# Buffers of the first expert's rows and of the side splits, and the engines that evacuate the output, in an attention and MoE kernel

## The chip, the cores and the metric

The kernel runs on one core of a Trainium2 chip, as one launch. The metric is the time of one execution on the device in microseconds; here it is given as the median of several runs. The engines that matter: TensorE (PE) multiplies into PSUM; ScalarE (ACT), VectorE (DVE) and GpSimd (POOL) copy, add and round; SyncE (SP) issues every DMA of this stage, in one queue and in program order. Each engine works through its own instructions in order, and waits on semaphores where an operand is not there or a buffer is not free.

## The reference

```python
def reference(**kwargs):
    attn_out = _attn_ref(**attn_kwargs)      # 4 x 8 x 576 x 64, window of 64
    x = ascontiguousarray(attn_out.transpose(0, 2, 1, 3)).reshape(2304, 512)
    return _moe_ref(x=x, **moe_kwargs)

def _moe_ref(x, w_gate, w1, w2):
    P = exp(x @ w_gate - max)                # 2304 x 8
    for _ in range(8):                       # Sinkhorn: rows, columns
        P /= P.sum(1, keepdims=True) + 1e-09
        P /= P.sum(0, keepdims=True) + 1e-09
        P *= N / E
    out = zeros((N, D))
    for e in range(8):                       # dense: all rows, all experts
        h = maximum(x @ w1[e], 0.0)          # 512 -> 1024
        out += P[:, e:e + 1] * (h @ w2[e])   # 1024 -> 512
    return out
```

## The kernel before

**Arithmetic.** Every product of 32-bit numbers is made of three products of rounded high and low parts; a "split" of a tile is a cast of its high part (ScalarE) and a subtraction for its low part (POOL). The two products of each expert are made by the seven-product scheme of Strassen and Winograd; the steps of a block are numbered 1 to 7 after the products and run in the order 1, 5, 6, 2, 7, 3, 4.

**Passes.** The 2304 rows are 18 tiles of 128, and three passes take six tiles each. Pass 0 splits the weights as it needs them and stores the splits of w1 in DRAM (w1d), and half of the combinations of w2 (w2d). Half of the first expert is computed in the attention phase already; its rows (yd, 128 x 512 a tile) are scaled by the gate and added when the outputs of a pass are finished. Only the passes 1 and 2 and the two places where a pass meets the next concern us.

**The flow of a pass.** First blocks F[0] to F[29] (L217: x times w1, TensorE; then scaling, rounding to a buffer G, three of them) and Second blocks S[u][0], S[u][1] for fifteen units u (L1148: G times w2 into the accumulator acc). The flow is F0; F1, F2, S0; F3, F4, S1; ...; F29, S14, and the last steps of a block are interlaced with the first of the next. In First.step, a product is copied from PSUM by ScalarE: qb (L1048) after product 1, p (L1053) after 5, u (L1060) after 6, r (L1070) after 2. A bank is written again three or four products later, so a late copy stops TensorE.

**Weights of S.** A unit needs seven parts of w2, each 128 x 512. load_w2 loads a raw part on SP into the ring wr (four buffers, L978); split_w2 casts it (L741, ScalarE) and subtracts it (L742, POOL) into one of eight split buffers (wp, w2c); the next split that comes up in the program issues the load owed for a buffer that has come free. w1's splits of F[i+2] are loaded by five DMAs after step 4 of F[i] (L754), and a change of expert brings two more (pb, the gate's row, L722).

**Side splits.** Pass 2's unit 0 takes its seven w2 parts already split, from w2keep in DRAM. Pass 1 makes them, one in each of the units 2 to 8: keep_split takes a raw part (a wr buffer) and a second wr buffer for its high half, casts (L998), subtracts (L999), and stores both (L1001), and the two buffers are loaded again once the stores have landed.

**Meetings.** Where one pass ends and the next begins, TensorE transposes each of six output tiles (turn, L1224) into a PSUM bank, and finish (L1233, VectorE) makes one operation of scaling the tile's first-expert row and adding the bank to it; flush stores it. At the second meeting (pass 1 to 2) rows 0 to 3 are loaded into the G buffer in which the next x stood (new_x, load_x, high L1250, low L1253), rows 4 and 5 into the two ys buffers. At the first meeting there is no first-expert row to add, and acc is stored as it stands (out_rows, L1209). At the end of pass 2 the last tiles are finished in pieces (even_tiles, after_last).

**Order.** It is written out by hand: hook(block, step) hangs a call behind a step of a block, prior does so for the next pass, and bulk and urgent are queues from which a step takes one or all.

Of the kernel before, what the change touches and what calls it, by code (L numbers as in the profile page):

```python
# [8 lines left out]
F32 = mybir.dt.float32  # L9
# [12 lines left out]
def window_attention_sinkhorn_moe(ctx: ExitStack, tc: tile.TileContext, q, k, v, w_gate, w1, w2, out):  # L22
# [300 lines left out]
    with tc.manual_schedule():  # L323
# [617 lines left out]
        with ExitStack() as p3:  # L941
# [19 lines left out]
            KEEP = {u: k for u, k in zip(range(2, 9), ORDER)}  # L961
            seq = []
            for p in range(1, NPASS):
                for u in range(n_units):
                    if p == 1 or u:
                        seq += [(p, u, k) for k in ORDER]
                    if p == 1 and u in KEEP:
                        seq += [("raw", 0, KEEP[u]), ("high", 0, KEEP[u])]
# [3 lines left out]
            def load_w2():  # L972
# [3 lines left out]
                t = new("wr", [P, 2, HD], F32R, 4)  # L976
                if p != "high":
                    nc.sync.dma_start(out=f32(t), in_=w2_block(u, part) if part < 3 else w2d[u][:, part - 3])  # L978
                R[p, u, part] = t

# [7 lines left out]
            def split_w2(p, u, part):  # L988
                while owed:
                    owed.pop(0)()  # L990
                W[p, u, part] = split_into(new_wp(), f32(R.pop((p, u, part))))
                owed.append(load_w2)

            def keep_split(part):
                while owed:
                    owed.pop(0)()
                r, h = R.pop(("raw", 0, part)), R.pop(("high", 0, part))
                nc.scalar.copy(out=h, in_=f32(r))  # L998
                nc.gpsimd.tensor_tensor(out=r, in0=f32(r), in1=f32(h), op=ALU.subtract)  # L999
                for x, t in enumerate((h, r)):  # L1000
                    nc.sync.dma_start(out=w2keep[part][:, :, x, :], in_=f32(t))  # L1001
                owed.extend([load_w2, load_w2])
# [208 lines left out]
            def load_y(p, ts, own=False):  # L1211
                for t in ts:
                    ys[t] = new("ys", [P, DM], F32, 2) if own else side["x"][:, ORDER[t]].rearrange("p k c -> p (k c)")[:, 0:DM]
                    nc.sync.dma_start(out=ys[t], in_=yd[FIRST[p] + t])

            ys, yps = {}, {}
# [15 lines left out]
            def finish(p, t, cols):  # L1232
                nc.vector.scalar_tensor_tensor(  # L1233
                    out=ys[t][:, cols], in0=ys[t][:, cols], scalar=prob[:, FIRST[p] + t, 0:1], in1=yps[t][:, cols], op0=ALU.mult, op1=ALU.add)
# [22 lines left out]
            next_pb(1, 1)  # L1257
            first = plans[0][1][0]
# [4 lines left out]
            for p, F, S, flow in plans:  # L1263
# [146 lines left out]
```

## Time and profile before

| | us |
|---|---|
| median of three runs | 1571.19 |
| fastest, slowest | 1570.77, 1574.69 |
| the profiled execution, its own time | 1571.05 |
| its span | 1569.3 |
| TensorE busy | 1549.7 (99%) |
| VectorE, POOL busy | 966.6 (62%), 985.3 (63%) |
| ScalarE busy | 759.3 (48%) |

The span is what the profiler recorded between the first and the last instruction; 1.75 us of the execution's own time lie around it. A busy TensorE is counted by its records, whose ends are modelled, so a group can seem to overlap with the next; the time of a product is better read from start to start. Pass 1 runs from about 668 us, the first meeting lies there, the second meeting is at about 1096 to 1160 us, and the last product ends at 1565.

### The profile page before, as it was taken

To read this page: it belongs to the slowest core of one execution; us is meant where nothing else is said; L and a number is where in the kernel's file an instruction comes from. 1 tells how busy PE (TensorE), PEld (TensorE's weight loads), DVE (VectorE), ACT (ScalarE), POOL (GpSimd) and SP (SyncE) were. 2 spreads that over 40 slices of the span, in tenths; PEclk is the share of its full clock that TensorE was granted. 3 is DMA by queue.
4 is the path that set the end of the run, shared out by engine and by line. 5 is a ranking of instruction groups with operands and counts; after the bars stand their busy time and mean duration, and the time that the engine had idled before them with its cause. 6 is when DMAs were issued, how large, how long until landed. Compare 5 with 4: busy or idle time off the path is not lost.

```text
span 1569.3 us, 26783 instructions
## 1 busy us (share of the span) xinstructions
PE 1549.7 (99%) x9665; PEld 1475.7 (94%) x9665; DVE 966.6 (62%) x1799; ACT 759.3 (48%) x1667; POOL 985.3 (63%) x920
## 2 busy tenths in 40 slices
PE   8999999999999999999999999999999999999998
PEld 7888889988998998899999999999999999999998
DVE  6666566575455455655665665665746566566666
ACT  6666535443443344355545545444454454454452
POOL 6244467677767677356676676566557666667564
PEclk9999999999999999999999999999999999999999
DMA  9876467567756765895666666665966566566562
GB/s 222 197 172 150 137 227 285 207 221 264 266 208 242 261 220 200 293 318 167 226 231 202 223 228 202 198 208 184 337 210 211 174 202 212 171 208 209 168 195 101
DMA packets 231233, 335.67 MB, mean 214 GB/s; under 512 B 70162, under 2 KB 153214, under 8 KB 227134
## 3 DMA queue, kind: packets, MB, share of 16 engines
q1 hardware_dynamic: 231102, 333.97, 65.7%
q8 instruction: 76, 1.25, 0.3%
q14 instruction: 55, 0.45, 0.1%
HBM read 236.34 MB, written 90.63 MB: 208 GB/s over the span
## 4 chain that ended last, share of the span: by engine, by line
PE 90%; DMA 4%; DVE 3%; ACT 2%; issue 1%; POOL 1%; SPq 0%; DVEq 0%; ACTq 0%
PE qb L217 17%; PE y L276 15%; PE qc L217 11%; PE qa L217 11%; PE qb L1148 10%; PE qa L1148 7%; PE qc L1148 7%; PE hp L562 3%; PE yp L576 3%; PE vp L479 1%; DMA w1c<-w1d 1%; PE sp L410 1%; PE tp L390 1%; PE tp L464 1%; DMA w2keep<-wr 1%
## 5 line engine op out<-in xcount | busy, mean ns | idle before, releaser
L217 PE MATMUL qb<-xc,w1c 128*128 128x384 f32 x1620 | 321.9, 336 | 4.1 <-ACT u L1060 3.5
L1034 POOL TENSOR_TENSOR G<-sm,G 128x384 fp32r<-128x384 f32 x176 | 179.2, 1018 | 186.3 <-ACT G L1030 186.3
L217 PEld LDWEIGHTS qb<-xc,w1c 128*128 128x128 f32 x1620 | 284.6, 188 | 6.3 <-ACT u L1060 5.1
L276 PE MATMUL y<-w2c,g 128*128 128x512 f32 x1080 | 251.2, 391 | 0.5 <-DVE acc L295 0.5
L276 PEld LDWEIGHTS y<-w2c,g 128*128 128x128 f32 x1080 | 201.8, 188 | 42.6 <-DVE acc L295 0.9
L217 PE MATMUL qa<-xc,w1c 128*128 128x384 f32 x1080 | 213.3, 337 | 0.2 <-DMA w1c<-w1d 0.2
L217 PE MATMUL qc<-xc,w1c 128*128 128x384 f32 x1080 | 213.0, 336 | 0.0
L217 PEld LDWEIGHTS qa<-xc,w1c 128*128 128x128 f32 x1080 | 190.4, 188 | 1.7 <-DMA w1c<-w1d 0.5
L217 PEld LDWEIGHTS qc<-xc,w1c 128*128 128x128 f32 x1080 | 190.1, 188 | 0.0
L1156 DVE TENSOR_TENSOR acc<-qb,acc 128x384 f32<-128x384 f32 x171 | 95.1, 556 | 123.8 <-PE qb L1148 116.8
L742 POOL TENSOR_TENSOR w2c<-wr,w2c 128x512 fp32r<-128x512 f32 x99 | 126.7, 1296 | 48.0 <-ACT w2c L741 38.0
L178 POOL TENSOR_TENSOR w2c<-stg,w2c 128x512 fp32r<-128x512 f32 x60 | 84.6, 1431 | 108.4 <-PE qb L217 95.8
L742 POOL TENSOR_TENSOR wp<-wr,wp 128x512 fp32r<-128x512 f32 x100 | 127.9, 1298 | 39.2 <-ACT wp L741 31.2
L1030 ACT CAST G<-sm 128x384 fp32r<-128x384 f32 x180 | 92.2, 513 | 65.7 <-DVE sm L1041 65.7
L1148 PE MATMUL qb<-G,w2c 128*128 128x384 f32 x552 | 111.4, 336 | 2.6 <-ACT qb L1162 2.6
L1148 PE MATMUL qb<-G,wp 128*128 128x384 f32 x528 | 106.5, 336 | 0.1
L1148 PEld LDWEIGHTS qb<-G,w2c 128*128 128x128 f32 x552 | 97.7, 188 | 2.9 <-ACT qb L1162 2.9
L295 DVE SCALAR_TENSOR_TENSOR acc<-y,prob,acc 128x512 f32<-128x512 f32 x72 | 54.0, 749 | 69.2 <-PE y L276 68.5
L1148 PEld LDWEIGHTS qb<-G,wp 128*128 128x128 f32 x528 | 93.5, 188 | 0.4 <-DVE G L1034 0.4
L1156 DVE TENSOR_TENSOR acc<-qc,acc 128x384 f32<-128x384 f32 x116 | 64.4, 555 | 41.3 <-PE qc L1148 40.7
L458 POOL TENSOR_TENSOR s<-s,rr 128x512 f32<-128x512 f32 x36 | 37.5, 1041 | 79.8 <-DVE rr L457 71.1
L1041 POOL TENSOR_TENSOR r<-sm,r 128x384 f32<-128x384 f32 x60 | 61.1, 1019 | 30.8 <-ACT u L1060 23.2
(205 smaller groups left out, 2918.0 us busy)
## 6 DMA issues: line engine op xcount, KB each, us to landing
w1c<-w1d SPq DMA_DIRECT2D x120, 512.0 KB, 6.4
w1d<-w1c SPq DMA_DIRECT2D x30, 1792.0 KB, 7.7
w1c<-w1d SPq DMA_DIRECT2D x180, 256.0 KB, 3.4
stg<-in_moe_w_dram SPq DMA_DIRECT2D x66, 512.0 KB, 4.2
wr<-w2d SPq DMA_DIRECT2D x118, 256.0 KB, 3.2
wr<-in_moe_w_dram SPq DMA_DIRECT2D x88, 256.0 KB, 3.2
w2d<-tf SPq DMA_DIRECT2D x30, 512.0 KB, 4.8
vs<-v SPq DMA_DIRECT2D x35, 128.0 KB, 4.2
```

The source lines that it names most:

```text
L178: nc.gpsimd.tensor_tensor(out=w[:, 1], in0=src[:, j], in1=f32(w[:, 0]), op=ALU.subtract)
L217: nc.tensor.matmul(bank, lhsT=w[:, ws, a, kk, :], rhs=xc[xs][:, b, kk, :], start=(first and j == 0), stop=(j == 5), skip_group_check=not f ...
L276: nc.tensor.matmul(yp, lhsT=g[:, a, o:o + P], rhs=w[:, x, :], start=(i == 0), stop=(i == 11))
L295: nc.vector.scalar_tensor_tensor(out=at, in0=yp, scalar=pr, in1=at, op0=ALU.mult, op1=ALU.add)
L562: nc.tensor.matmul(hp, lhsT=w1s[c][:, a, kk, :], rhs=xs[j][:, b, kk, :], start=(i == 0), stop=(i == 3 * KD - 1))
L576: nc.tensor.matmul(yp, lhsT=g[:, a, o * P:(o + 1) * P], rhs=w[:, x, :], start=(i == 0), stop=(i == 11))
L742: nc.gpsimd.tensor_tensor(out=t[:, :, 1, :], in0=r, in1=f32(t[:, :, 0, :]), op=ALU.subtract)
L1030: nc.scalar.copy(out=self.g[:, k, 0, :], in_=src)
L1034: eng.tensor_tensor(out=self.g[:, k, 1, :], in0=src, in1=f32(self.g[:, k, 0, :]), op=ALU.subtract)
L1041: eng.tensor_tensor(out=dst, in0=x, in1=y, op=op)
L1148: nc.tensor.matmul(bank, lhsT=W[p, u, wp][:, g, y, cols], rhs=G7[p, 2 * u + g][:, gp, x, :], start=(start and j == 0), stop=(j == 5), skip ...
L1156: nc.vector.tensor_tensor(out=at, in0=src, in1=at, op=ALU.add)
```

## The change

It alters five places.

1. The side splits take the two ys buffers in place of two wr buffers, and are three calls: the load behind step 4 of F[2u+2], the cast and the subtraction behind step 7 of S[u][0] (in before, taken from the queue bulk), the stores behind step 2 of S[u][1].
2. At the second meeting rows 2 to 5 lie in the wr ring, which then holds nothing else (the loads for pass 2's unit 1 are taken out and come back behind steps of F2), rows 0 and 1 in ys. The tiles turn in the order 2, 3, 4, 5, 0, 1, one step or more apart from before. Tiles 5 and 1 ("a") are copied by ScalarE from PSUM into the place of acc that they came from, their rows are scaled by POOL (scale_row) and added by POOL.
3. Of the next x, part 0 is rounded behind S[14][0].1 in place of S[14][1].1.
4. At the first meeting three of the six stores of acc are issued before the first block, and the split of w2 part 5 goes from F1.3 to F2.5.
5. At the end of the program tile 0's last three quarters are copied by ScalarE and added by POOL ("p"), in place of VectorE's one operation, and the whole row of that tile is scaled by POOL beforehand.

```diff
             KEEP = {u: k for u, k in zip(range(2, 9), ORDER)}
+            WR_ROWS = (2, 3, 4, 5)
             seq = []
             for p in range(1, NPASS):
                 for u in range(n_units):
                     if p == 1 or u:
                         seq += [(p, u, k) for k in ORDER]
-                    if p == 1 and u in KEEP:
-                        seq += [("raw", 0, KEEP[u]), ("high", 0, KEEP[u])]
+                if p + 1 < NPASS:
+                    seq += [(p, t, "row") for t in WR_ROWS]
...
-                if p != "high":
-                    nc.sync.dma_start(out=f32(t), in_=w2_block(u, part) if part < 3 else w2d[u][:, part - 3])
+                t = new("wr", [P, 2, HD], F32, 4)
+                if part == "row":
+                    ys[u] = t.rearrange("p a c -> p (a c)")
+                    nc.sync.dma_start(out=ys[u], in_=yd[FIRST[p] + u])
+                    return
+                nc.sync.dma_start(out=t, in_=w2_block(u, part) if part < 3 else w2d[u][:, part - 3])
                 R[p, u, part] = t
+
+            ys, yps = {}, {}
...
             def split_w2(p, u, part):
-                while owed:
+                while owed and seq and seq[0][2] != "row":
                     owed.pop(0)()
-                W[p, u, part] = split_into(new_wp(), f32(R.pop((p, u, part))))
+                W[p, u, part] = split_into(new_wp(), R.pop((p, u, part)))
                 owed.append(load_w2)
 
+            def load_kept(part):
+                raw_k[part] = r = new("ys", [P, DM], F32R, 2)
+                nc.sync.dma_start(out=f32(r), in_=w2_block(0, part) if part < 3 else w2d[0][:, part - 3])
+
             def keep_split(part):
-                while owed:
-                    owed.pop(0)()
-                r, h = R.pop(("raw", 0, part)), R.pop(("high", 0, part))
+                r, h = raw_k.pop(part), new("ys", [P, DM], F32R, 2)
                 nc.scalar.copy(out=h, in_=f32(r))
                 nc.gpsimd.tensor_tensor(out=r, in0=f32(r), in1=f32(h), op=ALU.subtract)
-                for x, t in enumerate((h, r)):
+                raw_k[part] = h, r
+
+            def store_kept(part):
...
                     nc.sync.dma_start(out=w2keep[part][:, :, x, :], in_=f32(t))
-                owed.extend([load_w2, load_w2])
+
+            raw_k = {}
 
             def load_split(p, part):
...
-                for t in ts:
-                    ys[t] = new("ys", [P, DM], F32, 2) if own else side["x"][:, ORDER[t]].rearrange("p k c -> p (k c)")[:, 0:DM]
+            def load_y(p):
+                for t in (0, 1):
+                    ys[t] = f32(new("ys", [P, DM], F32R, 2))
                     nc.sync.dma_start(out=ys[t], in_=yd[FIRST[p] + t])
 
-            ys, yps = {}, {}
+            def rows_in():
+                assert not bulk and len(owed) == len(WR_ROWS)
+                owed.clear()
+                for _ in WR_ROWS:
+                    load_w2()
+
+            def scale_row(p, t, cols):
+                nc.gpsimd.tensor_scalar(out=ys[t][:, cols], in0=ys[t][:, cols], scalar1=prob[:, FIRST[p] + t, 0:1], scalar2=None, op0=ALU.mult)
+
+            acc4 = acc.rearrange("p t d -> p (t d)").rearrange("p (k n c) -> p k n c", k=4, n=2)
 
             def turn(t, jh, bank=1):
                 o, n = divmod(t, 2)
@@ -1229,17 +1250,26 @@
...
+                if eng == "v":
+                    nc.vector.scalar_tensor_tensor(
+                        out=ys[t][:, cols], in0=ys[t][:, cols], scalar=prob[:, FIRST[p] + t, 0:1], in1=yps[t][:, cols], op0=ALU.mult, op1=ALU.add)
+                else:
+                    o, n = divmod(t, 2)
+                    k = slice(cols.start // P, cols.stop // P)
+                    nc.scalar.copy(out=acc4[:, k, n, o * P:(o + 1) * P], in_=yps[t][:, cols].rearrange("p (k c) -> p k c", c=P))
+                    y = ys[t][:, cols].rearrange("p (k c) -> p k c", c=P)
+                    if eng == "a":
+                        scale_row(p, t, cols)
+                    nc.gpsimd.tensor_tensor(out=y, in0=y, in1=acc4[:, k, n, o * P:(o + 1) * P], op=ALU.add)
                 r = (FIRST[p] + t) * P
                 stores.append(lambda t=t: nc.sync.dma_start(out=out[r:r + P, cols], in_=ys[t][:, cols]))
...
-            def turn_all(p, t, bank=1):
+            def turn_all(p, t, bank=1, eng="v"):
                 turn(t, ALL4, bank)
-                finish(p, t, slice(0, DM))
+                finish(p, t, slice(0, DM), eng)
...
                 load_w2()
             next_pb(1, 1)
+            out_rows(0, range(3))
             first = plans[0][1][0]
             first.step(1)
             first.step(5)
@@ -1270,8 +1301,8 @@
                     hooks.setdefault((blk, step), []).extend(fs)
 
                 if p == 1:
-                    hook(F[1], 6, lambda: out_rows(0, range(TP)))
-                    for (blk, st), k in zip(((F[1], 6), (F[1], 3), (F[2], 6)), range(4, 7)):
+                    hook(F[1], 6, lambda: out_rows(0, range(3, TP)))
+                    for (blk, st), k in zip(((F[1], 6), (F[2], 5), (F[2], 6)), range(4, 7)):
                         hook(blk, st, lambda p=p, k=k: split_w2(p, 0, ORDER[k]))
                 else:
                     for (blk, st), k in zip(((F[0], 6), (F[0], 2), (F[0], 7), (F[0], 3), (F[0], 4), (F[1], 6)), range(1, 7)):
...
                     if p == 1 and u in KEEP:
-                        hook(S[u][0], 1, lambda k=KEEP[u]: bulk.append(lambda: keep_split(k)))
+                        hook(F[2 * u + 2], 4, lambda k=KEEP[u]: load_kept(k))
+                        hook(S[u][0], 7, lambda k=KEEP[u]: keep_split(k))
+                        hook(S[u][1], 2, lambda k=KEEP[u]: store_kept(k))
...
                 if more:
                     hook(b, 3, lambda p=p: load_split(p + 1, ORDER[0]))
                     hook(F[n - 1], 6, lambda p=p: new_x(p + 1))
-                    for k, (blk, st) in zip(ORDER, ((a, 1), (b, 1), (a, 5), (a, 6), (b, 5), (b, 6), (a, 7))):
+                    for k, (blk, st) in zip(ORDER, ((b, 1), (b, 1), (a, 5), (a, 6), (b, 5), (b, 6), (a, 7))):
                         hook(blk, st, lambda k=k: (high(k), low(k, nc.gpsimd)))
-                    hook(a, 2, lambda p=p: load_y(p, range(4, TP), True))
-                    hook(b, 3, lambda p=p: load_y(p, range(4)))
+                    hook(F[n - 1], 6, lambda p=p: load_y(p))
+                    hook(a, 2, rows_in)
                     nf = plans[p][1]
-                    for t, (blk, st) in enumerate(((nf[0], 3), (nf[0], 4), (nf[1], 7), (nf[1], 4), (nf[2], 6), (nf[2], 7))):
-                        prior.setdefault((blk, st), []).append(lambda p=p, t=t: (flush(), turn_all(p, t)))
-                    for blk, st in ((nf[2], 1), (nf[2], 4)):
-                        prior.setdefault((blk, st), []).append(flush)
+                    for t, (blk, st), eng in zip((2, 3, 4, 5, 0, 1), ((nf[0], 6), (nf[0], 2), (nf[0], 3), (nf[1], 2), (nf[1], 4), (nf[2], 7)), "vvvava"):
+                        prior.setdefault((blk, st), []).append(lambda p=p, t=t, eng=eng: (flush(), turn_all(p, t, eng=eng)))
+                    prior.setdefault((nf[2], 4), []).append(flush)
+                    for st in (6, 3):
+                        prior.setdefault((nf[2], st), []).append(lambda: (load_w2(), load_w2()))
                 else:
 
                     def last_y(p=p):
@@ -1325,7 +1359,7 @@
 
                     def own_rows(p=p):
                         for t in (0, 2, 4):
-                            nc.gpsimd.tensor_scalar(out=ys[t][:, :P], in0=ys[t][:, :P], scalar1=prob[:, FIRST[p] + t, 0:1], scalar2=None, op0=ALU.mult)
+                            scale_row(p, t, slice(0, P if t else DM))
...
                             turn(t, ALL4[2:], bank)
                         for t in (0, 2, 4):
                             turn(t, ALL4[1:2])
-                            finish(p, t, slice(P, DM))
+                            finish(p, t, slice(P, DM), "v" if t else "p")
```

SP at unit 2 of pass 1, the side split's loads and stores; before, from the weights of F[6] on (w1c: splits of w1; wr: raw w2 part; w2keep: the store of the kept split):

```order
L754 DMA w1c_8384<-w1d_124 128x512 x3
L754 DMA w1c_8384<-w1d_124 128x1024 x2
L722 DMA pb_8390<-prow_102 128x3x128 x2
L978 DMA wr_8455<-w2d_156 128x512
L1001 DMA w2keep_146<-wr_8218 256x1x256
L1001 DMA w2keep_146<-wr_8206 256x1x256
L978 DMA wr_8468<-w2d_156 128x512
L978 DMA wr_8470<-in_moe_w_dram 128x2x256
L978 DMA wr_8482<-w2d_156 128x512
L978 DMA wr_8496<-in_moe_w_dram 128x2x256
```

After:

```order
L754 DMA w1c_8385<-w1d_124 128x512 x3
L754 DMA w1c_8385<-w1d_124 128x1024 x2
L722 DMA pb_8391<-prow_102 128x3x128 x2
L1002 DMA ys_8394<-in_moe_w_dram 128x2x256
L982 DMA wr_8461<-in_moe_w_dram 128x2x256
L982 DMA wr_8473<-w2d_156 128x512
L982 DMA wr_8485<-in_moe_w_dram 128x2x256
L1012 DMA w2keep_146<-ys_8436 256x1x256
L1012 DMA w2keep_146<-ys_8394 256x1x256
L982 DMA wr_8501<-w2d_156 128x512
L982 DMA wr_8529<-in_moe_w_dram 128x2x256
```

The kept part (ys_8394) is loaded behind the five weight loads and two pb loads of F[6]; the stores no longer stand ahead of three wr loads but behind them.

ScalarE at the same unit, before; the first row is the cast of the kept part:

```order
L998 CAST wr_8218<-wr_8206 128x512
L741 CAST wp_8472<-wr_8230 128x2x256
L741 CAST wp_8484<-wr_8455 128x2x256
L1048 COPY qb<-qa 128x384
L741 CAST wp_8498<-wr_8468 128x2x256
L1053 COPY p_0_8516<-qc 128x384
L741 CAST w2c_8526<-wr_8470 128x2x256
L741 CAST w2c_8538<-wr_8482 128x2x256
L1060 COPY u_0_8541<-qb 128x384
L741 CAST w2c_8550<-wr_8496 128x2x256
```

After:

```order
L1006 CAST ys_8436<-ys_8394 128x512
L741 CAST wp_8463<-wr_8206 128x2x256
L741 CAST wp_8475<-wr_8218 128x2x256
L741 CAST wp_8487<-wr_8231 128x2x256
L1060 COPY qb<-qa 128x384
L741 CAST w2c_8503<-wr_8461 128x2x256
L1065 COPY p_0_8521<-qc 128x384
L741 CAST w2c_8531<-wr_8473 128x2x256
L741 CAST w2c_8543<-wr_8485 128x2x256
L1072 COPY u_0_8546<-qb 128x384
L741 CAST w2c_8556<-wr_8501 128x2x256
```

The cast of the kept part stands where it stood, now with a load issued a block earlier as its source; the qb copy comes after three splits in place of two.

SP at the second meeting, before; yd are the first-expert rows:

```order
L729 DMA G_12060<-xd_t_101 128x768
L754 DMA w1c_12113<-w1d_117 128x512 x3
L754 DMA w1c_12113<-w1d_117 128x1024 x2
L722 DMA pb_12119<-prow_103 128x3x128 x2
L1214 DMA ys_12160<-yd_108 128x512
L1214 DMA ys_12162<-yd_109 128x512
L1006 DMA w2c_12246<-w2keep_146 128x1024
L1214 DMA G_12060<-yd_104 128x512
L1214 DMA G_12060<-yd_105 128x512
L1214 DMA G_12060<-yd_106 128x512
L1214 DMA G_12060<-yd_107 128x512
L1006 DMA w2c_12285<-w2keep_149 128x1024
```

After:

```order
L729 DMA G_12054<-xd_t_101 128x768
L1226 DMA ys_12062<-yd_104 128x512
L1226 DMA ys_12064<-yd_105 128x512
L754 DMA w1c_12111<-w1d_117 128x512 x3
L754 DMA w1c_12111<-w1d_117 128x1024 x2
L722 DMA pb_12117<-prow_103 128x3x128 x2
L980 DMA wr_12158<-yd_106 128x512
L980 DMA wr_12160<-yd_107 128x512
L980 DMA wr_12162<-yd_108 128x512
L980 DMA wr_12164<-yd_109 128x512
L1018 DMA w2c_12248<-w2keep_146 128x1024
L1018 DMA w2c_12289<-w2keep_149 128x1024
```

Rows 0 and 1 moved ahead of F0's weights, rows 2 to 5 from G and ys to wr, and the splits kept for unit 0 (w2keep) follow them.

## Rows read from the trace of the kernel before

**Rows 1.** Page, part 1: busy time, share of the span, instructions of each engine.
```profile
PE 1549.7 (99%) x9665; PEld 1475.7 (94%) x9665; DVE 966.6 (62%) x1799; ACT 759.3 (48%) x1667; POOL 985.3 (63%) x920
```

**Rows 2.** Waits of TensorE: engine, line, awaited; us in total, times, longest.
```profile
PE qb L217 <- ACT u L1060: 3.5, 5, 1.5
```

**Rows 3.** Timeline, first meeting: start, us of group, operation, count, idle before.
```profile
684.36 0.62 ACT L741 CAST wp<-wr 128x512 fp32r<-128x512 f32 x1
...
685.82 1.32 PE L217 MATMUL qb<-xc,w1c 128*128 128x384 f32 x6 [0.55 <-ACT qb L1048]
```

**Rows 4.** Timeline of TensorE behind the u copy, units 2 and 6.
```profile
770.66 1.14 PE L217 MATMUL qb<-xc,w1c 128*128 128x384 f32 x5 [0.55 <-ACT u L1060]
...
890.31 1.32 PE L217 MATMUL qb<-xc,w1c 128*128 128x384 f32 x6 [1.54 <-ACT u L1060]
```

**Rows 5.** Timeline of ScalarE at unit 2; and one row of SP's waits.
```profile
767.75 0.62 ACT L741 CAST wp<-wr 128x512 fp32r<-128x512 f32 x1 [3.81 <-DMA wr<-w2d]
...
770.14 0.47 ACT L1060 COPY u<-qb 128x384 f32<-128x384 f32 x1
...
SPq L978 <- DMA w2keep<-wr: 20.1, 7, 4.2
```

**Rows 6.** Timeline at the second meeting by engine; below, two stretches with granted clock.
```profile
1102.68 2.86 DVE L1034 TENSOR_TENSOR G<-sm,G 128x384 fp32r<-128x384 f32 x2 [0.82 <-ACT G L1030]
...
1102.97 2.15 POOL L1253 TENSOR_TENSOR xc<-G,xc 128x768 fp32r<-128x768 f32 x1
...
1104.45 1.58 PE L1148 MATMUL qb<-G,wp 128*128 128x384 f32 x6
...
1124.89 0.66 PE L1224 MATMUL y<-ident,acc 128*128 128x128 f32 x4 [0.38 <-DVE G L1233]
...
1143.35 0.48 ACT L1030 CAST G<-qa 128x384 fp32r<-128x384 f32 x1 [5.67 <-DMA out_dram<-G]
...
1144.68 1.40 PE L1148 MATMUL qb<-G,w2c 128*128 128x384 f32 x6 [2.62 <-ACT qb L1162]
1145.87 2.12 PE L1148 MATMUL qa<-G,wp 128*128 128x384 f32 x6
1147.79 1.86 PE L1148 MATMUL qa<-G,w2c 128*128 128x384 f32 x6
1149.48 0.69 PE L1148 MATMUL qb<-G,wp 128*128 128x384 f32 x3
...
888.00:891.00 3.00, 1.46 (x9) 1.14 (x8) 0.31 (x1) 2.99 (x7) 2.56 (x3) 1.00 0.47 165
...
1146.00:1149.00 3.00, 3.00 (x11) 3.00 (x10) 2.66 (x6) 2.08 (x6) 1.91 (x3) 0.50 0.95 284
```

**Rows 7.** Timeline at the end of the program.
```profile
1562.62 1.66 DVE L1233 SCALAR_TENSOR_TENSOR G<-G,prob,yt 128x384 f32<-128x384 f32 x3 [0.42 <-PE yt L1224]
...
1564.54 0.72 PE L1353 MATMUL y<-ident,acc 128*128 128x128 f32 x3 [0.68 <-DVE acc L1185]
```

**Rows 8.** Groups of POOL by line: busy us, mean ns of one, idle before.
```profile
L999 POOL TENSOR_TENSOR wr<-wr,wr 128x512 fp32r<-128x512 f32 x7 | 9.0, 1285 | 0.0
...
L1328 POOL TENSOR_SCALAR G<-G,prob 128x128 f32<-128x128 f32 x3 | 1.8, 610 | 0.0
```

**Rows 9.** Timeline of SP: loads before the side splits of units 2 and 5.
```profile
752.39 2.22 SPq L754 DMA_DIRECT2D w1c<-w1d  x5
...
755.90 1.77 SPq L978 DMA_DIRECT2D wr<-w2d  x1
...
841.79 2.22 SPq L754 DMA_DIRECT2D w1c<-w1d  x5
```

**Rows 10.** Landing of wr loads: issued at 755.90; at 844.11; the two near 1002.
```profile
DMA to landing us min/median/max: 7.0/7.0/7.0
...
DMA to landing us min/median/max: 7.1/7.1/7.1
...
DMA to landing us min/median/max: 2.9/3.0/3.1
```

More of the change, by code (lines that the diff above doesn't have):

```diff
@@ L975, in load_w2 @@
                 p, u, part = seq.pop(0)
-                t = new("wr", [P, 2, HD], F32R, 4)
-                if p != "high":
-                    nc.sync.dma_start(out=f32(t), in_=w2_block(u, part) if part < 3 else w2d[u][:, part - 3])
+                t = new("wr", [P, 2, HD], F32, 4)
[4 more added lines that the diff above has]
+                nc.sync.dma_start(out=t, in_=w2_block(u, part) if part < 3 else w2d[u][:, part - 3])
                 R[p, u, part] = t
+            ys, yps = {}, {}
             def new_wp():
@@ L988, in split_w2 @@
             def split_w2(p, u, part):
-                while owed:
+                while owed and seq and seq[0][2] != "row":
                     owed.pop(0)()
-                W[p, u, part] = split_into(new_wp(), f32(R.pop((p, u, part))))
+                W[p, u, part] = split_into(new_wp(), R.pop((p, u, part)))
                 owed.append(load_w2)
+            def load_kept(part):
+                raw_k[part] = r = new("ys", [P, DM], F32R, 2)
+                nc.sync.dma_start(out=f32(r), in_=w2_block(0, part) if part < 3 else w2d[0][:, part - 3])
             def keep_split(part):
-                while owed:
-                    owed.pop(0)()
-                r, h = R.pop(("raw", 0, part)), R.pop(("high", 0, part))
+                r, h = raw_k.pop(part), new("ys", [P, DM], F32R, 2)
                 nc.scalar.copy(out=h, in_=f32(r))
                 nc.gpsimd.tensor_tensor(out=r, in0=f32(r), in1=f32(h), op=ALU.subtract)
-                for x, t in enumerate((h, r)):
+                raw_k[part] = h, r
+            def store_kept(part):
+                for x, t in enumerate(raw_k.pop(part)):
                     nc.sync.dma_start(out=w2keep[part][:, :, x, :], in_=f32(t))
-                owed.extend([load_w2, load_w2])
+            raw_k = {}
             def load_split(p, part):
@@ L1209, in out_rows @@
                     nc.sync.dma_start(out=out[(FIRST[p] + t) * P:(FIRST[p] + t + 1) * P, :], in_=acc[:, t, :])
-            def load_y(p, ts, own=False):
-                for t in ts:
-                    ys[t] = new("ys", [P, DM], F32, 2) if own else side["x"][:, ORDER[t]].rearrange("p k c -> p (k c)")[:, 0:DM]
+            def load_y(p):
+                for t in (0, 1):
+                    ys[t] = f32(new("ys", [P, DM], F32R, 2))
                     nc.sync.dma_start(out=ys[t], in_=yd[FIRST[p] + t])
-            ys, yps = {}, {}
+            def rows_in():
[6 more added lines that the diff above has]
+            acc4 = acc.rearrange("p t d -> p (t d)").rearrange("p (k n c) -> p k n c", k=4, n=2)
             def turn(t, jh, bank=1):
@@ L1230, in flush, with finish @@
                     stores.pop(0)()
-            def finish(p, t, cols):
-                nc.vector.scalar_tensor_tensor(
-                    out=ys[t][:, cols], in0=ys[t][:, cols], scalar=prob[:, FIRST[p] + t, 0:1], in1=yps[t][:, cols], op0=ALU.mult, op1=ALU.add)
+            def finish(p, t, cols, eng="v"):
+                if eng == "v":
[9 more added lines that the diff above has]
+                    nc.gpsimd.tensor_tensor(out=y, in0=y, in1=acc4[:, k, n, o * P:(o + 1) * P], op=ALU.add)
                 r = (FIRST[p] + t) * P
```

## The prediction

> **What bounds the kernel now.** I read the page's first part first: TensorE is busy 99% of the span [rows 1]. Time can only be won where TensorE stands still or runs at half clock, and a change that adds a few hundred rows of work elsewhere costs nothing until TensorE waits for one of them. So the second view is the list of TensorE's waits, whose largest entry is the u copy of ScalarE, five stops [rows 2]; the third is the timeline at each stop. A group of six 128x384 products takes 1.04 us from start to start. A stop costs its bracket, plus about 0.16 us in which the modelled end of the last product runs on, plus about 0.1 us until products follow one another closely again. I add 0.26 to each bracket. The change touches four places.
>
> *First meeting.* qb waits 0.55 for a ScalarE copy that stood behind the split of a w2 part [rows 3]: 0.8 with the 0.26.
>
> *Side splits of pass 1.* Five stops, 3.5 us of brackets [rows 2], with five times 0.26 a loss of 4.8. One reads it at unit 2: products start at 770.66 behind a bracket of 0.55 [rows 4], so their slot was free at 769.95, since the u copy ended only at 770.61 [rows 5]. ScalarE stood 3.81 us until 767.75 for a w2 part [rows 5], whose load waited on SP for the w2keep store to release its buffer: seven such waits, 20.1 us [rows 5]. Two of the four wr buffers are tied up by the kept part and its high half.
>
> *Second meeting.* The largest piece is at 1144.68, 2.62 us [rows 6]: the copy stands behind a ScalarE cast that waited 5.67 us for an out_dram store out of G, the buffer in which rows 0 to 3 of the first expert lie. Then the clock falls: a granted clock of 0.50 in 1146 to 1149, and the groups at 1145.87 and 1147.79 take 1.92 and 1.69 us from start to start in place of 1.04 [rows 6], 1.5 lost, 1.7 with the third. At 1104.45 a group is followed after 1.61 us: the TensorE operand comes from VectorE's G<-sm, two of which took 2.86 us beside the x low of POOL [rows 6]. 1124.89 waits 0.38 for a row's evacuation by VectorE [rows 6].
>
> *End.* TensorE waits 0.68 at 1564.54 for VectorE's adds, which stand behind three evacuations of 1.66 us together [rows 7].
>
> **The change part by part.**
>
> *A, first meeting.* The split goes from F1.3 to F2.5, behind the copy. ScalarE's copy then starts when its product ends, and the stop of 0.8 goes. Three of the six output stores go out before the first weights of F1, so those are issued later on SP by three issues. Bounds: -1.2 (the neighbouring wait for w1c goes too) and +0.5 (w1c comes that much later). I take **-0.8**.
>
> *B, second meeting.* Rows 2 to 5 lie in the wr ring, 0 and 1 in ys; G is free when the x lows end, so the cast at 1143.35 finds its buffer free and the stop at 1144.68 and the half clock go: 2.62 + 0.26 + 1.7 = 4.6. The x high and low of part 0 leave the step behind which VectorE stood at 1104: 0.6 of the 1.61. The evacuations of rows stand at other steps and three are left on VectorE besides one of row 0: the 0.38 + 0.16 at 1124.89 goes. 4.6 + 0.6 + 0.5 = 5.7. The new work: two rows, copied by ScalarE, scaled and added by POOL. POOL's 128x512 subtraction takes 1.285, and four 128x128 scalings at 0.610 would make 2.4 [rows 8]; so 1.3 to 2.4 for the scale, I take 1.3 (its width is nearer), and 1.3 for the add. A row has the rest of its flow step until its store, so this is covered by the products that run meanwhile; if the cover is gone, the next casts of G by POOL come up to 3.7 late, and TensorE with them. A second new wait is on SP: row 2's load stands behind the weights and pb of F0 in the queue. A load behind five w1c issues and pb took 7.0 [rows 10], and VectorE's evacuation of row 2 is the first of all. By the same distance the row lands about as TensorE finishes its turn; a us later it holds VectorE, not TensorE. Bounds: -6.2 (a smaller stop in front of it goes too) and -2 (row 2 and the scales together give back two stops of 1.5 to 2). I take **-5.7**.
>
> *C, end.* One of three evacuations, 1.66 / 3 = 0.55, goes from VectorE to ScalarE's copy and POOL's add. VectorE's adds then wait for their own product instead, which ended about 0.35 before them. Bounds -0.57 and +0.3 (POOL's add, three quarters of 1.285, ends last). I take **-0.4**.
>
> *D, side splits.* The wr buffers are no longer tied up, and no wr load waits for a store. The 4.8 would be gone; but two things are placed anew. The load of the kept part now stands on SP behind the five weight loads of F[2u+2], which wait for TensorE, and for u = 2, 4, 6, 8 behind two pb loads too. And ScalarE's cast of it stands ahead of the three ready wp splits, qb, p and u. Both are order, not speed: whoever is late holds the whole of ScalarE, and POOL's subtraction holds POOL's splits in the same way.
> When does the load land? In the trace of before a wr load stands at this place of the queue. Unit 2: w1c issued at 752.39, wr at 755.90 [rows 9], landed 7.0 later [rows 10], so at 762.9, or 10.5 after the first w1c. Of the four pb units three read 10.5, unit 4 reads 11.1. Without pb: w1c at 841.79, five issues of 2.22 [rows 9], wr at 844.1, landed 7.1 later [rows 10], 9.4 after.
> What follows the landing L? ScalarE's cast 0.62 [rows 5]. POOL: kept subtraction and the subtractions of parts 1 and 2, three at about 1.29 [rows 8], L + 4.5. Only then is the buffer of part 2 free and part 6 loaded into it, 2.9 to 3.1 on a quiet queue [rows 10]: L + 7.5. ScalarE splits part 6 in 0.62 and copies u in 0.47 [rows 5], so u ends at L + 8.6; each operation starts about 0.1 before the modelled end of the one ahead, so I take L + 8.4.
> When is u due? The slot at 769.95 is 17.56 after the first w1c. So the stop is L - w1c + 8.4 - 17.56: 10.5 gives 1.4, 11.1 gives 2.0, 9.4 gives 0.2. Four pb units: 1.4, 2.0, 1.4, 1.4; three others: 0.2 each; together 6.8, and 0.1 each to run closely again: 7.5, where 4.8 stood. **+2.6** (7.5 less the 4.87 that the five stops cost from start to start). Bounds: -4.9, if the load lands some 1.4 us earlier than the old wr load did (that had to wait for its buffer first), and +7, if all four come out longer and cost clock as well.
>
> Sum: -0.8 - 5.7 - 0.4 + 2.6 = -4.3. The profiled execution took 1571.05, so 1566.75; it lies 0.14 under the median of the runs, 1571.19, so 1566.9 at most. I say **1566.7**, 0.29% below the median. A measurement of this kernel tells about 0.3% from no change (1566.5 and 1575.9).
>
> **The rivals.**
>
> *R1: the side splits stop nothing.* For it: the old wr load at 755.90 spent 1.77 on SP [rows 9], some of it waiting for its buffer, which ys does not; against it: the next landing, in the units without pb, is as long (7.1) without such a wait. If it holds, D is -4.9: -0.8 - 5.7 - 0.4 - 4.9 = -11.8, 1559.3.
>
> *R2: slower.* TensorE's clock falls in the four pb units. The one stop of 2.62 is followed by a granted clock of 0.50, the one of 1.54 at 890.31 [rows 4] by 1.00 in its stretch [rows 6]. If each of the four stops is about 2.5 in place of 1.5, and each costs the 1.7 behind 1144.68 too, D is 2.6 + 4 x (1.0 + 1.7) = 13.4: with A, B and C 1577.6. It decides from a landing 1 us later than the old one. Against it: nothing that the trace shows makes the load longer than the one in its old place.
> The Trainium skill, TensorE: Matmul & The Clock Gate, section Part 1: The HAM clock gate, says that the clock is at its half level by default and that sustained activity releases it. By that rule any stop can be followed by the half level; the rows after 1144.68 agree (0.50, that is 1.2 GHz), those after 890.31 do not.
>
> *R3: the second meeting keeps half.* Row 2 late on VectorE, or POOL's scales long. VectorE then gives back two stops of 1.5 to 2: B is -2.5, sum -1.1, 1570.
> POOL and VectorE also get in each other's way here: VectorE's two G<-sm took 2.86 and ended at 1105.54, 0.4 behind the end of POOL's x low at 1105.12 [rows 6].
> The Trainium skill, SBUF — State Buffer, section SBUF: two separate sides, says that GpSimd and a VectorE operation with two SBUF inputs lock each other out of a shared port, for the whole length of an instruction. The trace agrees (2.86 us for two operations). By that rule each of the new scales and adds can hold such a VectorE operation back, which is one way to R3.
>
> *R4: the rows' buffers don't free G,* since something else holds it until 1143: then the B of 5.7 is 1.1 and the time 1571.3. The order shows no other reader of G there; 3 in 100.
>
> **How the numbers follow.** The forecast, D between +0.5 and +5 and B near -5.7: 0.55, 1564.5 to 1569. R1 0.20, 1559.3 to 1563. R3 and R4 0.17. R2 0.08. Range 1559.0 to 1572.0: it leaves out R2 and some of the ends. Faster by over 0.3%: R1, and somewhat under half of the forecast: 0.46. Slower by over 0.3%: R2, 0.08. Within: 0.46.
>
> **What would show it.** A: no bracket at ScalarE's qb copy in the first meeting. B: no TensorE idle near 1140, no half clock behind it, G casts on ScalarE waiting for nothing. C: the last idle before y 0.3. D: in seven units ScalarE waits on the ys load, and the first products behind the u copy of F[2u+3] stop by 1.4 to 2.0 in units 2, 4, 6, 8 and 0.2 in 3, 5, 7. I am wrong if the ys loads land under 9 us behind the first w1c issue (R1), if the granted clock falls in the pb units (R2), or if VectorE's evacuations wait on rows (R3).

## The result and the profile after

| | median, us | lowest to highest | ratio to before, 95% interval |
|---|---|---|---|
| before | 1570.76 | 1569.69 to 1574.69 (6 runs) | |
| after | 1581.82 | 1576.46 to 1584.26 (6 runs) | 1.0062 [1.0043, 1.0081] |
| forecast | 1566.7 | 1559.0 to 1572.0 | |

The change makes the kernel slower by 0.6 to 0.7%, and its runs spread over 8 us. The profiled execution took 1579.0, its span is 1577.3 (1569.3 before): it shows 8 of the 11 us that lie between the medians. The mean granted clock was 0.998 in the shortest run of the kernel after (1576.5), 0.996 in the profiled one and 0.993 to 0.995 in the four of 1581.7 to 1584.3, so these spent more time at half clock, in line with the other 3 us. TensorE's busy time is 1.6 longer than in [rows 1], so 6.4 of the 8 us are idle time. The list of TensorE's waits of the kernel after (us in total, times, longest) has one that grew by more than 1 us, the one of [rows 2]:

```profile
PE 1551.3 (98%) x9665; PEld 1477.2 (94%) x9665; DVE 960.6 (61%) x1796; ACT 760.6 (48%) x1670; POOL 991.8 (63%) x925
```

```profile
PE qb L217 <- ACT u L1072: 12.1, 9, 2.8
...
PE y L1387 <- DVE acc L1197: 0.4, 1, 0.4
```

The wait of qb L1148 for ScalarE, 2.62 at 1144.68 in [rows 6], is not in the list any more; the last row is the end of the program, 0.38 where [rows 7] has 0.68.

To place the loss I take, from the trace, the time between the starts of successive products, and add up what exceeds the usual distance by over 0.06 us (a stop, the first product behind one, each product at half clock), by stretch of the program:

| lost, us | first meeting (640-700) | side splits (700-1000) | second meeting (1090-1200) | end (from 1200) |
|---|---|---|---|---|
| before | 1.3 | 4.9 | 6.8 | 1.2 |
| after | 0.7 | 20.6, of it 4.4 half clock | 0.6 | 0.9 |
| difference | -0.6 | +15.8 | -6.2 | -0.3 |
| forecast | -0.8 | +2.6 | -5.7 | -0.4 |

The differences add up to 8.7, where the spans differ by 8.0. Three of the four terms hold within half a us. The one that was forecast with the wrong size is D, the side splits. Here are four of its stops in the timeline of TensorE after, at units 4, 5, 6 and 8:

```profile
836.32 1.67 PE L217 MATMUL qb<-xc,w1c 128*128 128x384 f32 x6 [2.84 <-ACT u L1072]
...
868.49 1.31 PE L217 MATMUL qb<-xc,w1c 128*128 128x384 f32 x6 [1.07 <-ACT u L1072]
...
900.45 1.32 PE L217 MATMUL qb<-xc,w1c 128*128 128x384 f32 x6 [2.01 <-ACT u L1072]
...
964.83 1.31 PE L217 MATMUL qb<-xc,w1c 128*128 128x384 f32 x6 [2.36 <-ACT u L1072]
```

and the stretches behind the stops of units 2, 4, 6, 8 (stretch, its length, busy time and count of the engines, granted clock, DMA share, GB/s):

```profile
772.00:775.00 3.00, 3.00 (x12) 3.00 (x11) 1.07 (x2) 1.25 (x3) 1.09 (x2) 0.54 0.83 290
837.00:840.00 3.00, 3.00 (x11) 3.00 (x10) 1.43 (x3) 1.71 (x5) 1.27 (x2) 0.51 0.75 268
902.00:905.00 3.00, 3.00 (x11) 3.00 (x10) 1.17 (x3) 1.56 (x4) 0.87 (x1) 0.50 0.59 186
965.00:968.00 3.00, 3.00 (x18) 3.00 (x19) 1.18 (x3) 1.47 (x4) 1.52 (x2) 1.00 0.81 257
```

In 3 us TensorE does 18 products at full clock and 11 at half. Three of these four stops are followed by half clock, which costs about 1.5 us each. Unit 2 shows the way from the late load to the stop. SP, in its order:

```profile
754.56 1.78 SPq L1002 DMA_DIRECT2D ys<-in_moe_w_dram  x1
756.44 0.81 SPq L982 DMA_DIRECT2D wr<-in_moe_w_dram  x1
765.34 0.34 SPq L982 DMA_DIRECT2D wr<-w2d  x1
766.60 0.37 SPq L982 DMA_DIRECT2D wr<-in_moe_w_dram  x1
767.02 1.18 SPq L1012 DMA_DIRECT2D w2keep<-ys  x2
768.30 1.22 SPq L982 DMA_DIRECT2D wr<-w2d  x1
```

ScalarE, then POOL, then TensorE:

```profile
762.06 0.62 ACT L1006 CAST ys<-ys 128x512 fp32r<-128x512 f32 x1 [5.13 <-DMA ys<-in_moe_w_dram]
762.59 1.66 ACT L741 CAST wp<-wr 128x512 fp32r<-128x512 f32 x3
...
770.58 0.62 ACT L741 CAST w2c<-wr 128x512 fp32r<-128x512 f32 x1 [1.51 <-DMA wr<-in_moe_w_dram]
771.11 0.47 ACT L1072 COPY u<-qb 128x384 f32<-128x384 f32 x1
773.75 0.62 ACT L741 CAST w2c<-wr 128x512 fp32r<-128x512 f32 x1 [2.18 <-DMA wr<-w2d]
...
762.76 1.30 POOL L1007 TENSOR_TENSOR ys<-ys,ys 128x512 fp32r<-128x512 f32 x1 [4.27 <-DMA wr<-in_moe_w_dram]
764.01 3.81 POOL L742 TENSOR_TENSOR wp<-wr,wp 128x512 fp32r<-128x512 f32 x3
...
771.63 1.81 PE L217 MATMUL qb<-xc,w1c 128*128 128x384 f32 x6 [2.66 <-ACT u L1072]
```

The kept part lands at 762.04, the cast starts at once, the three splits that were ready stand behind it (762.59), and so do POOL's. The load of the sixth part goes out at 766.60, 4.6 after the landing, when POOL has freed its buffer. Its cast waits for it until 770.58, and only then comes the u copy, which ends at 771.58. u was due at 768.81 (the start at 771.63 less the stop of 2.82 from start to start). The seventh part (768.30), behind the two stores, holds its cast until 773.75.

At the second meeting there is neither a long stop nor half clock (compare [rows 6]), and ScalarE's G cast, which waited 5.67 us for a store out of G before, waits for nothing:

```profile
1143.06 0.48 ACT L1042 CAST G<-qa 128x384 fp32r<-128x384 f32 x1
...
1143.00:1146.00 3.00, 3.00 (x20) 2.96 (x20) 2.93 (x7) 2.93 (x8) 2.92 (x4) 1.00 0.97 339
1146.00:1149.00 3.00, 3.00 (x19) 3.00 (x18) 1.90 (x5) 1.84 (x5) 3.00 (x5) 1.00 1.02 376
```

### The profile page after: what moved, and what is told of

Read it like the earlier page. It is cut to its first block, busy times and chain, and to the rows that moved or that the text cites. A ratio compares the mean times of both kernels' runs of the same rounds, so it can differ in the third digit from the quotient of the medians.

```text
span 1577.3 us, 26781 instructions
## 1 busy us (share of the span) xinstructions
PE 1551.3 (98%) x9665; PEld 1477.2 (94%) x9665; DVE 960.6 (61%) x1796; ACT 760.6 (48%) x1670; POOL 991.8 (63%) x925
## 4 chain that ended last, share of the span: by engine, by line
PE 88%; DMA 5%; DVE 2%; issue 2%; POOL 1%; ACT 1%; SPq 1%; DVEq 0%; POOLq 0%; ACTq 0%
PE qb L217 17%; PE y L276 15%; PE qc L217 11%; PE qa L217 10%; PE qb L1160 10%; PE qa L1160 7%; PE qc L1160 7%; PE hp L562 3%; PE yp L576 3%; DMA wr<-in_moe_w_dram 2%; PE vp L479 1%; PE tp L390 1%; DMA wr<-w2d 1%; PE sp L410 1%; PE tp L464 1%
## 5 line engine op out<-in xcount | busy, mean ns | idle before, releaser
L217 PE MATMUL qb<-xc,w1c 128*128 128x384 f32 x1620 | 323.7, 337 | 12.7 <-ACT u L1072 12.1
L217 PE MATMUL qc<-xc,w1c 128*128 128x384 f32 x1080 | 216.8, 340 | 0.0
L217 PEld LDWEIGHTS qc<-xc,w1c 128*128 128x128 f32 x1080 | 194.0, 191 | 0.0
L1053 DVE TENSOR_TENSOR y<-qb,p 128x384 f32<-128x384 f32 x60 | 34.0, 566 | 78.4 <-PE qb L217 76.9
```

The source lines that it names most:

```text
L217: nc.tensor.matmul(bank, lhsT=w[:, ws, a, kk, :], rhs=xc[xs][:, b, kk, :], start=(first and j == 0), stop=(j == 5), skip_group_check=not f ...
```

## The experiments

All runs are of edits of the two kernels; every ratio is to runs of the kernel before that were taken beside them, whose medians were 1572.40 (first four kernels) and 1571.27 (last four).

**The load one block earlier.** Theory: what counts is that the part lands behind its turn. Rival: the extra operations ahead of the unit's splits are too long in themselves.

```diff
-                        hook(F[2 * u + 2], 4, lambda k=KEEP[u]: load_kept(k))
+                        hook(F[2 * u + 1], 4, lambda k=KEEP[u]: load_kept(k))
```

> The changed kernel with one edit: the load of the kept part stands one First block earlier (behind step 4 of F[2u+1] in place of F[2u+2]), so ahead of F[2u+2]'s five weight loads and two gate loads. Cast, subtraction and stores stay where they are. Theory (the late landing holds ScalarE and POOL in order): the part lands some 7 us before its cast, the seven stops behind the u copy (0.0 to 3.0 us, 12 us with three falls of the clock worth 4.4) go, and so do the small ones that follow them; the sum lost between 700 and 1000 us falls from 20.6 to under 1, and the time to about 1571 - 0.6 (first meeting) - 6.2 (second) - 0.3 (end) - 4.9 (old side splits) = 1559, 1558 to 1562. Rival (the two extra operations ahead of the unit's splits, 0.6 on ScalarE and 1.3 on POOL, are too long themselves, wherever the load is): the stops stay near 2 us in the units whose expert changes, 1575 or more.

1558.58 (1558.26 to 1558.77), ratio 0.9917 [0.9903, 0.9932]. The lost time of the side splits is 0.0. At unit 2 the part lands 3.3 us ahead of its cast; the 7 that I expected left out that the cast, which waits for nothing now, runs at its turn, some 5 us earlier. ScalarE, then TensorE:

```profile
756.65 0.62 ACT L1006 CAST ys<-ys 128x512 fp32r<-128x512 f32 x1
757.17 1.66 ACT L741 CAST wp<-wr 128x512 fp32r<-128x512 f32 x3
...
766.76 0.48 ACT L1072 COPY u<-qb 128x384 f32<-128x384 f32 x1 [0.58 <-PE qb L217]
...
768.62 1.20 PE L217 MATMUL qb<-xc,w1c 128*128 128x384 f32 x6
```

The same operations in the same order on ScalarE and POOL, and u ends 1.4 us before its bank is needed. So the two operations are not too long; the rival falls. The kernel is faster than the kernel before by 0.83%, and than the kernel after by about 1.5%; its four runs lie within 0.5 us where those of the kernel after spread over 8.

**The load late, but nothing behind it.**

```diff
-                        hook(S[u][0], 7, lambda k=KEEP[u]: keep_split(k))
-                        hook(S[u][1], 2, lambda k=KEEP[u]: store_kept(k))
...
+                    if p == 1 and u in KEEP:
+                        hook(S[u][1], 3, lambda k=KEEP[u]: bulk.append(lambda: keep_split(k)))
+                        hook(F[2 * u + 4], 2, lambda k=KEEP[u]: store_kept(k))
```

> The changed kernel with the load of the kept part left where it is, late, but its cast and subtraction put behind the unit's seven splits in the order of ScalarE and POOL, and its stores one block later. Theory (order, not transfers): though the part lands as late as before, nothing of the unit's own splits stands behind it, no stop behind the u copy is left, 1559 to 1563. Rival (the load, or the 512 KB more traffic in this stretch, delays the unit's own loads): the stops remain in part, 1567 to 1578.

1558.81 (1558.49 and 1559.13), ratio 0.9919 [0.9899, 0.9939], lost time of the side splits 0.0. ScalarE at unit 2 and TensorE's next start:

```profile
766.88 0.48 ACT L1072 COPY u<-qb 128x384 f32<-128x384 f32 x1 [0.58 <-PE qb L217]
...
769.68 0.63 ACT L1006 CAST ys<-ys 128x512 fp32r<-128x512 f32 x1
...
768.73 1.20 PE L217 MATMUL qb<-xc,w1c 128*128 128x384 f32 x6
```

The load stands where it stands in the kernel after, and its data is late for the place where that kernel casts it. It does no harm, since the cast now stands behind the u copy. The edit moves the stores back too; that moving the stores alone does not remove the long stops is shown further down. Late data and a place ahead of others make the loss together; taking away either removes all of it.

**Half a dose: the load ahead of the gate loads.**

```diff
+                for u in KEEP if p == 1 else ():
+                    hook(F[2 * u + 2], 4, lambda k=KEEP[u]: load_kept(k))
                 for i in range(1, n):
                     e = groups[i][0]
...
                     if p == 1 and u in KEEP:
-                        hook(F[2 * u + 2], 4, lambda k=KEEP[u]: load_kept(k))
```

> The changed kernel with the load of the kept part ahead of the two gate loads (pb) in units 2, 4, 6 and 8, but still behind the five weight loads: half a dose. Theory (the stop grows one for one with the landing): the part lands about 1.0 us earlier in these four units (two pb issues took 0.96), their stops fall from 2.8, 3.0, 2.2, 2.5 to about 1.8, 2.0, 1.2, 1.5, units 3, 5, 7 keep 0 to 1.2, and with no stop over 2.1 the granted clock stays at 1.00 behind them: 4 for the stops and 4.4 for the clock off the time, about 1573, 1570 to 1576. Rival (the landing is not what decides): 1579 to 1584 as before.

1573.98 (1570.04 to 1577.29, 10 runs), ratio 1.0014 [1.0001, 1.0026]. The time is the expected one, by another composition, as far as the profile tells: it shows the fastest of the ten runs (1570.04), and the 4 us up to the median are not placed. In the four units the part lands 9.5, 9.1, 9.3 and 9.1 after the first weight issue in place of 10.8, 11.4, 10.9 and 10.6: 1.3 to 2.3 earlier, more than the 1.0 I took. The stops there fall to 0.6, 0.3, 1.0 and 0.0, and no stretch shows half clock. But 7 of the 11.2 us that this profile still loses are small stops behind these, which I had not counted. The waits of TensorE, then ScalarE, TensorE and SP at unit 3:

```profile
PE qb L217 <- ACT u L1072: 4.7, 11, 0.8
PE qb L217 <- ACT qb L1060: 1.2, 4, 0.4
```

```profile
802.78 0.62 ACT L741 CAST w2c<-wr 128x512 fp32r<-128x512 f32 x1 [2.70 <-DMA wr<-w2d]
...
808.39 1.34 PE L217 MATMUL qb<-xc,w1c 128*128 128x384 f32 x6 [0.41 <-ACT u L1072]
...
796.39 1.18 SPq L1012 DMA_DIRECT2D w2keep<-ys  x2
797.67 0.56 SPq L982 DMA_DIRECT2D wr<-w2d  x1
```

The seventh part is loaded behind the two stores (797.67) and is there 5.1 us later (802.78). ScalarE waits for it ahead of the G casts of the block, which end later, and so the next block's u copy at 807.87, too.

**The stores behind the loads.**

```diff
-                        hook(S[u][1], 2, lambda k=KEEP[u]: store_kept(k))
+                        hook(F[2 * u + 3], 2, lambda k=KEEP[u]: store_kept(k))
```

> The changed kernel with the two stores of the kept part behind the load of the unit's seventh part and of the next two, in place of ahead of the seventh. It tests the size I missed: the load of the sixth part took 2.7 to 4.0 us to land where I reckoned 3.0, with the two stores issued 0.4 and 1.0 behind it. If the stores slow it: it lands in 2.7 to 3.1 in all seven units, the four long stops shrink by about 1 us each and keep the clock: about 1572, 1569 to 1575. If not (the load's own time varies): it still takes up to 4.0 and the time stays at 1578 to 1584.

1573.98 (1571.89 to 1578.30, 10 runs), ratio 1.0011 [0.9998, 1.0025]: 8 us under the kernel after, about the time expected if the stores slow the sixth part, but mostly not for that reason. The sixth part's load took 2.8 to 2.9 us in five units and 3.7 and 3.6 in units 2 and 8. In the kernel after it was 4.0, 2.9, 3.7, 3.7, 3.3, 2.7, 3.9. So in units 4, 5 and 6 moving the stores took off 0.4 to 0.9 us; in units 3 and 7 the stores had cost nothing, and in units 2 and 8 most of the extra time stays, for a reason that was not found. The long stops stay, at 2.6, 2.6, 2.1 and 2.5 in the pb units, and unit 7 has one of 1.3:

```profile
PE qb L217 <- ACT u L1072: 10.4, 6, 2.4
```

because in units 4, 6, 7 and 8 the landing, counted from the first weight issue, became later (12.1, 11.2, 10.5 and 10.9, where the kernel after has 11.4, 10.9, 9.4 and 10.6); in unit 2 the sixth part's load alone keeps the stop. SP now has the stores ahead of the weights of the next block; that this is the reason was not tried. What the edit does remove are the small stops behind the seventh part (one of 0.3 us is left): that part now lands after 3.2 to 3.6 us, in place of 4.9 to 5.6 behind the stores. And half clock stands behind one stop only (1.5 us in place of 4.4).

**The side splits alone, on the kernel before.** The part of the diff with load_kept, keep_split, store_kept and their three hooks, and nothing else.

> The kernel before with the side splits' part of the change alone: ys buffers, late load, cast ahead of the unit's splits. If the loss of the changed kernel is all in this part and the parts do not touch each other: the stops behind the u copy cost about 15.8 us more than the kernel before has there (20.6 in place of 4.9), so about 1586, 1580 to 1590, wide since the clock falls behind some of the long stops only. Rival (the loss needs the other parts too, by another phase of the loads): 1570 to 1578.

1590.97 (1587.68 to 1593.91), ratio 1.0122 [1.0102, 1.0143]. The lost time between 700 and 1000 us is 23.7, of it 5.9 half clock. It is a us over the range I gave; the second meeting loses 9.0 in this profile, 2.2 more than before, in the old stop:

```profile
PE qb L1152 <- ACT qb L1166: 3.7, 1, 3.7
```

**All but the side splits.** The kernel after with the old keep_split, its two wr buffers and its place in bulk.

> The changed kernel with the old side splits: two wr buffers, cast from the queue, wr reloads behind the stores. All other parts stay. If the parts add up: 1571 - 0.6 (first meeting) - 6.2 (second) - 0.3 (end) = 1563.9, 1562.5 to 1565.5, with the old five stops of together 4.9 us between 700 and 1000 us and none at the second meeting. Rival (the gain at the second meeting hangs on the freed wr buffers of the side splits): 1567 or more.

1563.08 (1559.86 to 1563.88), ratio 0.9941 [0.9924, 0.9958]. TensorE waits for u as in [rows 2], and for nothing at the second meeting:

```profile
PE qb L217 <- ACT u L1069: 3.8, 4, 1.5
```

Lost at the side splits 5.5, at the second meeting 0.5. So the rest of the change does what was forecast for it without the side splits. The two halves add up: +1.22% for the side splits alone and -0.59% for all the rest make +0.63%, and the whole change measured +0.62%.

**Which half of the second meeting.** The kernel with the early load, and "vvvvvv" in place of "vvvava".

> The kernel with the early load (e1), but all six rows of the second meeting evacuated by VectorE; the buffers and the steps stay. If the buffers alone make the gain there: within 1 us of that kernel's 1558.6 (1558.3 to 1559.6). If the two evacuations on ScalarE and POOL carry it: 1560.5 or more, with a stop of TensorE behind the evacuation of tile 5 or 1.

1559.65 (1559.26 to 1560.24), ratio 0.9924 [0.9909, 0.9939]; 1.1 us over the kernel with the early load, a little beyond the bound set for "the buffers alone", far from 6. One stop came back, and the loss at that meeting is 1.0 in place of 0.5:

```profile
1123.11 1.15 PE L217 MATMUL qb<-xc,w1c 128*128 128x384 f32 x5 [0.23 <-DVE y L1053]
```

So the gain there comes from the buffers and the order of the steps, which this run leaves together, and the two evacuations on ScalarE and POOL make 0.5 us of it by the profile, 1.1 by the times, which were taken beside different runs of the kernel before.

**First meeting and end as before,** on the kernel with the early load.

> The kernel with the early load (e1), but the first meeting's order and the program's end as in the kernel before. By the sums of lost time, 0.3 in place of 1.3 at the first meeting and 0.9 in place of 1.2 at the end: 1.3 us longer than that kernel's 1558.6, 1559.3 to 1560.4. If neither part does anything: 1558.3 to 1558.9.

1560.48 (1559.90 to 1560.78), ratio 0.9929 [0.9913, 0.9946]: 1.9 us over the kernel with the early load, in the direction expected and 0.1 beyond the range. The profile shows 0.5 of it at the first meeting (0.8 in place of 0.3, the stop of [rows 3] again) and 0.3 at the end; the remaining us is not placed.

## Why the prediction was wrong, point by point

**What bounds the kernel.** Right: every us that the profile places lies in a stop of TensorE or in the clock behind one.

**A, -0.8: right in kind, -0.6.** The split now stands behind ScalarE's copy (685.17), and TensorE's wait of 0.55 in [rows 3] is gone. The copy does not start when its product ends, as I had it, but behind a cast; 0.7 us of small stops stay. ScalarE, then TensorE after:

```profile
683.79 0.52 ACT L1042 CAST G<-sm 128x384 fp32r<-128x384 f32 x1
684.20 0.48 ACT L1060 COPY qb<-qa 128x384 f32<-128x384 f32 x1
...
685.17 0.62 ACT L741 CAST wp<-wr 128x512 fp32r<-128x512 f32 x1
...
684.74 1.32 PE L217 MATMUL qb<-xc,w1c 128*128 128x384 f32 x6
```

**B, -5.7: right, -6.2.** G is free when the casts come; no half clock. POOL's scale, of which only 128 columns could be read ([rows 8]), is 1.58, nearer to the lower of the bounds 1.3 and 2.4, and hidden:

```profile
L1235 POOL TENSOR_SCALAR wr<-wr,prob 128x512 f32<-128x512 f32 x1 | 1.6, 1582 | 0.0
```

R3 did not come: no row was late on VectorE, and the operations of POOL beside VectorE's held TensorE nowhere. R4 falls with the stop at 1144, which went when the rows left G.

**C, -0.4: right, -0.3.** TensorE's wait at the end went from 0.68 to 0.38.

**D, +2.6: the step that failed; it measured +15.8.** The mechanism was forecast: a late part, ScalarE and POOL held in order, part 6 loaded late, u late. The landing was forecast well too: 10.5, 9.4 and 11.1 after the first weight issue, measured 10.6 to 11.4 with pb and 9.4 to 9.5 without. What was too small, and what was left out (landings read at the start of the kept part's cast, stops from start to start of the products):

| unit | landing after first w1c issue | part 6's load, to its cast | u ends after the landing | stop forecast | stop measured |
|---|---|---|---|---|---|
| 2 | 10.8 | 4.0 | 9.5 | 1.4 | 2.8, half clock behind it |
| 3 | 9.4 | 2.9 | 8.4 | 0.2 | 0.3 |
| 4 | 11.4 | 3.7 | 9.2 | 2.0 | 3.0, half clock behind it |
| 5 | 9.5 | 3.7 | 9.2 | 0.2 | 1.2 |
| 6 | 10.9 | 3.3 | 8.8 | 1.4 | 2.2, half clock behind it |
| 7 | 9.4 | 2.7 | 8.3 | 0.2 | 0.2 |
| 8 | 10.6 | 3.9 | 9.4 | 1.4 | 2.5 |

The formula itself, landing plus the end of u behind it less 17.56, gives every measured stop of this table, and of the half dose, within 0.1. What was wrong are the numbers put into it, and what was left out beside it. D's stretch lost 20.6 where 7.5 was forecast; of the 13.1 between them about 5.5 are point 1, 3.2 point 2 and 4.4 point 3.

1. The term "2.9 to 3.1 on a quiet queue" was 2.7 to 4.0. With it "u ends at L + 8.4" became L + 8.3 to L + 9.5, worth 4.0 us in all; landings up to 0.4 later are worth 1.3. The stops are 12.3 us in place of 6.8. The queue was not quiet: the part's own stores go out 0.4 and 1.0 us behind that load. They explain some of it (units 4 to 6 in the run with the stores behind the loads), not all (units 2 and 8). The trace of before had shown a busy queue in these very units: there four wr loads go out some 0.5 us behind one another, and the twenty of them that can be read took 3.4 to 4.7 us (4.7 for the one issued at 765.76). I had taken two loads near 1002 that stand 1.2 us apart.
2. The small stops behind the seventh part, 3.2 us in this profile, were not in the sum. The diff and the order showed that the stores stand ahead of the seventh part's load; I costed the sixth part and stopped.
3. The half clock, 4.4 us, was in a rival (R2) and not in the sum. R2's sign came, the granted clock fell in three of the four pb units, and its price of 1577.6 is 1.4 under the profiled execution and 4 under the median. But it did not come by R2's condition, a landing 1 us later: the landings were 0.1 to 0.4 later, and the sixth part's load made the stops long. That R2's price comes near is partly luck, since it had a fall in all four units and no small stops. I gave it 0.08, since the stop of 1.54 in [rows 4] kept the clock and I put the new ones at 1.4 to 2.0. (The stretch that I read for it, 888 to 891 in [rows 6], ends 0.7 us behind that stop; the trace has no half clock after it either, so the reading holds.) From 1.4 to the row of 2.62 that did lose it was about one us, the uncertainty of the load that I had priced by one quiet row.

R1 did not come for this kernel: no kept part landed under 9 us behind the first weight issue. Its price is what the early load shows: 1559.3 forecast, 1558.6 measured. The parts A, B and C with the loss of D at zero add up.

## What to carry to other kernels

In this kernel a split whose source was loaded late cost nothing where nothing stood behind it; put ahead of other work on an in-order engine, it delayed all of that work, and the loads whose buffers that work frees. So give a load that has no urgency a whole block of lead, or give its consumer the last place; either alone was worth 23 us here. Price a load by rows in which the queue is as busy as it will be, not by one that stands alone, and follow the order to the last load behind it. And where a stop is forecast within a us of stops after which the clock fell, put that fall into the sum with a chance to match, not at a few per cent.

## What the runs showed of the hardware

- Stops of like size were followed by either level of the clock. In the kernel after, brackets of 2.66, 2.84 and 2.01 us were followed by a granted clock of 0.50 to 0.54, one of 2.36 by 1.00. In the kernel with the stores behind the loads, a bracket of 2.39 at 770.95 was followed by 0.52 and one of 2.40 at 834.51 by 1.00. The Trainium skill, TensorE: Matmul & The Clock Gate, section Part 1: The HAM clock gate, ties the level to TensorE's activity; the trace agrees in that each fall of the kernel after between 640 and 1560 us stands behind a stop, but the length of the stop alone does not say which level follows.
- The kernels without a stop behind the u copy spread by 1 us or less over two to four runs, the others by 4 to 8. The half dose is one of these (7 us over ten runs), though its profile has no stop over 1.0 and no half clock behind one, and its granted clock does not go with its time (0.998 in a run of 1576.0); what spreads its runs stays open.
- A POOL scaling of 128x512 by a scalar for each partition takes 1.57 to 1.58 us, a POOL addition of the same size 1.29: the operation with one array operand is the slower of the two.
- One 256 KB load took 2.7 to 4.0 us with two stores of the same size issued behind it, and one issued behind the two stores 4.9 to 5.6 (kernel after, seven units). With the stores moved back these were 2.8 to 3.7 and 3.2 to 3.6.
